# Converting six channel-mix weight parts before the last key/value batch is done, with part of its lerp and square work moved to DVE and three raw key/query tiles

## The chip, the cores and the metric

One NeuronCore of a Trainium2 chip runs the whole program. The metric is the device time of one execution in microseconds; the kernel before takes 1013.36 us (median of three runs, 1012.07 to 1013.84).

## What is computed

Three layers follow each other on a batch of 4, a sequence of 576 and 512 features: rotary attention with 8 heads, a channel mix with a gate, and a token mix followed by a wider channel mix.

```
q_rot, k_rot = rotate(q), rotate(k)
attn = softmax(q_rot @ k_rot^T / 8)
x    = attn @ v                                  # [4, 576, 512]

xk = mu_k * x + (1 - mu_k) * x_prev              # x_prev: x shifted by one position
xr = mu_r * x + (1 - mu_r) * x_prev
k  = relu(xk @ w_k)
y  = sigmoid(xr @ w_r) * ((k * k) @ w_v)         # [4, 576, 512]

h  = relu(y^T @ w_tok1) @ w_tok2                 # token mix, 576 -> 256 -> 576
u  = y + h^T
out = u + relu(u @ w_ch1) @ w_ch2                # channel mix, 512 -> 1536 -> 512
```

All weights arrive as 64-bit floats (read as pairs of 32-bit words), everything else as 32-bit floats.

## The kernel before, in words

**Precision.** Every operand of a large matmul is split into a high and a low half, both of type fp32r, and a product is three matmuls: high·high, high·low, low·high (`mm3`, L535 to L539). One matmul has 128 rows, 128 columns of weights and 288 columns of data (half a sequence), so that all units below come in halves `c` = 0, 1.

**Attention.** There are 16 groups `g` (4 batches, 4 head pairs) of 9 steps each, so 144 steps. A step makes scores (`emit_S`, L370), their maximum (L376, DVE), the exponential (L383, ACT), the normalized high half (L75, ACT) and low half (L402, DVE), and sends both through a DMA transpose (L417, L419) on the SP queue; twice per group the transposed tiles meet the values on PE (`emit_pv`, L432), and the result goes to `xT` (L82, DVE) and to memory `xd`. The raw key and query tiles, two of each per group (`rk`, `rq`, loaded by `ld_raw`, L263 and L266), are rotated in place on POOL and split (`split_hi`, `split_lo`). `BUFS` says how many raw tiles there are: 4 and 4.

**Key/value and gate units.** `kvr_gen` makes, for a batch and half, a K unit: four lerp slices (`lerp_slice`, one per 128 features), eight products `kp` with `w_k`, relu (`t`, L606, ACT), square (`k2`: high half L610 on ACT, `q` and the low half on POOL), and four products `vp` with `w_v`, whose results go to memory `vd`. An R unit makes four lerp slices and four products `rp` with `w_r`, the sigmoid (L650) and its multiplication into `y`. K units of batches 0 to 2 run between the steps of attention; then come, in this order (`SEQ`), K(3,0), R(0,0), R(0,1), K(3,1). A lerp slice is five instructions in a chain: `a` on POOL (L77), `f` scaled on ACT (L75), `f` plus `a` on POOL (L104), the high half `xs` on ACT (L73), the low half on POOL (L104). There is one buffer for `a`, one for `f`, four for `xs`.

**Weights.** `Conv` brings a part of a weight matrix (128 rows by 512 words of 64 bits, 512 KB; `w_tok1` 256 wide, `w_tok2` 576 wide) from memory to the place where its two halves will stand, and converts it by an absolute value on ACT (L191), four instructions on DVE (L196, L198, L200, L203), a copy to the high half on ACT (L73) and a subtraction for the low half on DVE (L104, written as `parts`). `conv0` does `w_k` and `w_v` during the first four groups of attention. `conv1` does `w_r` (4 parts), `w_tok1` (5), `w_tok2` (2). `conv2` does `w_ch1` and `w_ch2`, 12 parts each, in blocks of four.

**Where things lie.** The pools of attention (rk, rq, the rotation table, sp with the split keys and queries, and so on) are a stack on the right side of SBUF, opened in this order. When they are closed, the pools of the next stage (`top`: the three conversion buffers cv, then `w_r`, `w_tok1`, `w_tok2`, y, ...) are opened from the same end, so each takes the room of some attention pools and waits for the last reader there. The pools of the key/value stage (`wrk`, `kvs`) lie on the left.

**Order.** The program is written as generators that are advanced in turn; a scheduler then fixes each engine's instruction order ahead of the run, from priorities and its own estimates. On the chip each engine runs its list strictly in that order, and the SP queue issues its DMAs strictly in order too, so an instruction that waits holds up all behind it.

**The end.** After R(0,1), the token mix of batch 0 (`tok_gen`: `trp`, `ytk`, `t1p`, `t2p`) runs beside K(3,1). Then `ch_gen` does the channel mix of all batches (`uhl` splits, `c1p`, `hs`, `co`), with the gates and token mixes of batches 1 to 3 (`pre_gen`) in between. `PRE_FROM` and `PRE_EARLY` say from which channel item on, and how far per item, that work is advanced while weights are still being converted.

Of the kernel before, what the change touches and what calls it, by code (L numbers as in the profile page):

```python
# [33 lines left out]

SEQ = [("K", 3, 0), ("R", 0, 0), ("R", 0, 1), ("K", 3, 1)]

KVN, TKN, PRE, PRE_EARLY, PRE_FROM = 5, 6, 20, 6, 6

BUFS = dict(rk=4, rq=4, sp=2, vr=2, v16=2, p16=4, pt=2, sm=4, sc=3, la=1, lf=1, xs=4, t=2, q=2, vt=2)

PRI = dict(den=50, hi=400, pv=20, ld=-100, v=-50, low=50, rope=200, conv1=20, kv=-200, kvpe=-200)

# [22 lines left out]
def body(tc, kin, qin, vw, tabs, ident, mu, w_k, w_v, w_r, w_t1, w_t2, w_c1, w_c2, out):  # L65
# [37 lines left out]
    def tt(e, o, a, b, op):  # L103
        return (pool if e == "P" else dve).tensor_tensor(o, a, b, op=op)  # L104

    ctx = ExitStack()
    with ctx:
# [35 lines left out]
        def w3(w):  # L143
            return w.rearrange("(k p) f -> p k f", p=128)
# [377 lines left out]
        @prio("lerp")  # L522
        def lerp_slice(x, o, kk, w):
            a = P["a"].tile([128, HS], F32, tag="a", name="a")
            copy("P", a, x[:, kk, o:o + HS], om_s[:, w, kk:kk + 1])
            f = P["f"].tile([128, HS], F32, tag="f", name="f")
            copy("A", f, x[:, kk, o + 1:o + HS + 1], mu_s[:, w, kk:kk + 1])
            tt("P", f, f, a, ALU.add)
            t = P["xs"].tile([128, 2, HS], F32R, tag="xs", name="xs")
            copy("A", t[:, 0], f)  # L530
            tt("P", t[:, 1], f, t[:, 0].bitcast(F32), ALU.subtract)
            return t

        def mm3(p, w, m, t, first, last):
# [14 lines left out]
        def kvr_gen(seq, ready):  # L549
# [31 lines left out]
            for n, (kind, b, c) in enumerate(seq):  # L581
# [12 lines left out]
                if kind == "K":  # L594
                    k2 = [None] * KF
                    for m in range(KF):
                        p = accps("kp")
                        for kk in range(KD):
                            with ahead(PRI["kvpe"]):
                                mm3(p[:, 0:HS], wk[m // 4][kk], m % 4, xs[kk], kk == 0, kk == KD - 1)  # L600
                            tick()
                            yield 3

                        def ev1(p=p, m=m):
                            k2[m] = P["t"].tile([128, HS], F32, tag="t", name="t")
                            act.activation(out=k2[m], in_=p[:, 0:HS], func=AF.Relu)  # L606

                        def ev2(m=m):
                            t, k2[m] = k2[m], P["k2"].tile([128, 2, HS], F32R, tag="k2", name="k2")
                            act.activation(out=k2[m][:, 0], in_=t, func=AF.Square)  # L610
                            q = P["q"].tile([128, HS], F32, tag="q", name="q")
                            tt("P", q, t, t, ALU.mult)
                            tt("P", k2[m][:, 1], q, k2[m][:, 0].bitcast(F32), ALU.subtract)
                        later((1, ev1), (2, ev2))
                    load(n + 1)
                    for m in range(KD):
                        p = accps("vp")
                        for kf in range(KF):
                            with ahead(PRI["kvpe"]):
                                mm3(p[:, 0:HS], wv[kf // 4][kf % 4], m, k2[kf], kf == 0, kf == KF - 1)  # L620
                            if kf == 1:
                                load(n + 1)
                            if kf == 4:
                                lerp(n + 1)
                            tick()
                            yield 3

                        def ev(p=p, m=m, b=b, c=c):
                            vt = P["vt"].tile([128, HS], F32, tag="vt", name="vt")
                            copy("A", vt, p[:, 0:HS])  # L630
                            sp.dma_start(vd[b][c][:, m], vt)
                        later((1, ev))
                else:
                    load(n + 1)
                    y = u_of[b]
                    cc = slice(c * HS, (c + 1) * HS)
                    sp.dma_start(y[:, :, cc], vd[b][c])
                    for m in range(KD):
                        p = accps("rp")
                        for kk in range(KD):  # L640
                            with ahead(PRI["kvpe"]):
# [12 lines left out]
                        later((1, ev))  # L654
# [118 lines left out]
        def top(nm, bufs, st=mw):  # L773
            return st.enter_context(tc.tile_pool(name=nm, bufs=bufs, side="right"))
# [5 lines left out]
        y_p = [top("y0", 1)]  # L780
        M["ytk"], M["h1"] = top("m_ytk", 1), top("m_h1", 1)

        def cv_t():
            return cv_p.tile([128, S], I32, tag="cv", name="cv")

        cv = Conv(cv_t, [wr, t1, t2], "conv1", low="D")
        u_of[0] = y_p[0].tile([128, KD, S], F32, tag="y", name="y")
        for _ in range(3):
            cv.step()
# [1 line left out]
        while not kv.done:  # L791
            kv.advance(30)
            if not cv.done():
                cv.step()
            elif r_done:
                if tok is None:
                    tok = Stream(tok_gen(0))
                tok.advance(TKN)
# [6 lines left out]
        c1_w, c2_w = [], []
        for o in range(0, KC, 4):
            c1_w.append(Weights(top(f"c1{o}", 1), [w3(w_c1)[:, k, 128 * o:128 * o + 512] for k in range(KD)],
                                [128, 2, 512]))
            c2_w.append(Weights(top(f"c2{o}", 1), [w3(w_c2)[:, o + k] for k in range(4)], [128, 2, DM]))
# [5 lines left out]
        mi_p = mx.enter_context(tc.tile_pool(name="mi_p", bufs=2, space=PS))  # L815
        c1_p = mx.enter_context(tc.tile_pool(name="c1_p", bufs=2, space=PS))
        co_p = mx.enter_context(tc.tile_pool(name="co_p", bufs=4, space=PS))
        cv = Conv(cv_t, [w for ws in zip(c1_w, c2_w) for w in ws], "conv2", low="D")

        def gate_gen(b):  # L820

# [33 lines left out]
        def ch_gen():  # L855
# [3 lines left out]
            for n in range(len(items) + LAG):  # L859
# [18 lines left out]
                if n >= LAG:  # L878
                    b, c, kf = items[n - LAG]
                    h = hs_of.pop(n - LAG)  # L880
                    for m in range(KD):
                        if kf == 0:
                            co_of[m] = co_p.tile([128, 512], F32, tag="co", name="co")
                        mm3(co_of[m][:, 0:HS], c2_w[kf // 4][kf % 4], m, h, kf == 0, kf == KC - 1)
                    if kf == KC - 1:
                        cc = slice(c * HS, (c + 1) * HS)
                        for m in range(KD):
# [13 lines left out]
        while not ch.done:  # L901
# [73 lines left out]
```

## Time and profile before

| what | value |
|---|---|
| median of three runs | 1013.36 us (1012.07 to 1013.84) |
| the profiled execution's own time | 1011.27 us |
| its span in the trace | 1009.5 us |
| PE busy | 897.5 us, 89% of the span |
| DVE / ACT / POOL busy | 56% / 48% / 44% |
| mean granted TensorE clock | 0.949 |

A row of the timeline gives start, duration, engine, line, operation, output and inputs, and in brackets how long the engine had been idle and which instruction ended that. A row of the table by stretches gives, for each engine, its busy time in that stretch and in parentheses how many instructions began there, then the granted TensorE clock, the share of the DMA engines and what they moved. Matmuls overlap in the records (a record lasts 0.29 us, the next begins 0.13 us later), so a stretch with no idle time may still hold fewer matmuls than it could.

### The profile page before, as it was taken

How to read it: one execution, taken by the hardware profiler on the slowest of the kernel's cores; microseconds unless marked ns; L12 is line 12 of the kernel's file. 1: busy time of each engine (PE TensorE's matmuls, PEld its weight loads, DVE VectorE, ACT ScalarE, POOL GpSimd, SP SyncE). 2: the span in 40 equal slices, each digit the busy share in tenths (PEclk: the TensorE clock that was granted, in tenths of full speed). 3: DMA queues.
4: the chain of work that ended last, by engine and by line, in shares of the span. 5: the costliest groups of instructions: out<-in, count | busy, mean ns of one | idle time of the engine just before them, and what ended most of it. 6: DMA issues, size and time to landing. Idle time of an engine off the chain costs nothing.

```text
span 1009.5 us, 17679 instructions
## 1 busy us (share of the span) xinstructions
PE 897.5 (89%) x6544; PEld 822.2 (81%) x6544; DVE 566.3 (56%) x1237; ACT 487.9 (48%) x1088; POOL 445.5 (44%) x484
## 2 busy tenths in 40 slices
PE   2566578999998899989888888999999999999998
PEld 1454456788787788878787788999999999999997
DVE  5998987768677577796850199932223211231111
ACT  2665666767677586766554455541133112221110
POOL 6679866857768654452567731240141013101010
PEclk9965577999999999999999999999999999999999
DMA  7999888898788877687920283020120002000000
GB/s 252 289 269 237 163 167 169 184 182 174 177 176 173 156 133 149 153 191 134 215 95 24 67 314 148 13 60 1 39 62 22 21 2 77 1 24 15 10 25 24
DMA packets 212054, 120.80 MB, mean 120 GB/s; under 512 B 175232, under 2 KB 192768, under 8 KB 211840
## 3 DMA queue, kind: packets, MB, share of 16 engines
q1 hardware_dynamic: 211968, 119.67, 50.1%
q8 instruction: 52, 0.85, 0.4%
q14 instruction: 34, 0.28, 0.1%
HBM read 60.90 MB, written 14.16 MB: 74 GB/s over the span
## 4 chain that ended last, share of the span: by engine, by line
PE 55%; DVE 5%; DMA 3%; POOL 2%; ACT 2%; issue 1%; SPq 0%; DVEq 0%; POOLq 0%; ACTq 0%
PE c1p L537 5%; PE co L537 5%; PE c1p L538 5%; PE c1p L539 5%; PE co L538 5%; PE co L539 5%; PE S L370 4%; PE pv L432 2%; PE vp L537 2%; PE kp L537 2%; PE vp L538 2%; PE vp L539 2%; PE rp L537 1%; PE rp L538 1%; PE rp L539 1%; PE kp L539 1%
## 5 line engine op out<-in xcount | busy, mean ns | idle before, releaser
L370 PE MATMUL S<-kq 64*128 64x288 f32 (+1 forms) x864 | 154.4, 341 | 26.3 <-DVE p L402 18.0
L370 PEld LDWEIGHTS S<-kq 64*128 64x128 f32 (+1 forms) x864 | 123.9, 213 | 50.0 <-issue 26.3
L383 ACT ACTIVATE S<-S,nm 128x576 f32<-128x576 f32 x144 | 102.2, 713 | 66.9 <-DVE nm L376 66.1
L874 DVE SCALAR_TENSOR_TENSOR hs<-c1p,hs 128x288 fp32r<-128x288 f32 x96 | 43.8, 456 | 152.5 <-ACT hs L873 152.1
L376 DVE TENSOR_REDUCE nm<-S 128x1 f32<-128x576 f32 x144 | 106.6, 751 | 38.9 <-PE S L370 38.3
L402 DVE SCALAR_TENSOR_TENSOR p<-S,rc,p 128x576 f16<-128x576 f32 x144 | 114.3, 811 | 19.3 <-ACT p L75 17.7
L873 ACT ACTIVATE hs<-c1p 128x288 fp32r<-128x288 f32 x96 | 38.8, 409 | 171.0 <-PE c1p L539 167.7
L104 POOL TENSOR_TENSOR uhl<-y,uhl 128x288 fp32r<-128x288 f32 x32 | 26.4, 852 | 212.8 <-ACT uhl L73 212.5
L537 PE MATMUL c1p<-uhl,parts 128*128 128x288 f32 x384 | 114.6, 299 | 3.7 <-DVE y L104 3.7
L538 PE MATMUL c1p<-uhl,parts 128*128 128x288 f32 x384 | 114.4, 298 | 0.0
L539 PE MATMUL c1p<-uhl,parts 128*128 128x288 f32 x384 | 114.4, 299 | 0.0
L539 PE MATMUL co<-hs,parts 128*128 128x288 f32 x384 | 112.6, 296 | 0.0
L538 PE MATMUL co<-hs,parts 128*128 128x288 f32 x384 | 112.5, 296 | 0.0
L75 ACT ACTIVATE p<-S,rc 128x576 f16<-128x576 f32 x144 | 104.4, 749 | 13.4 <-ACT S L383 4.4
L537 PE MATMUL co<-hs,parts 128*128 128x288 f32 x384 | 107.7, 296 | 0.0
L537 PE MATMUL kp<-xs,parts 128*128 128x288 f32 x256 | 79.8, 322 | 14.6 <-ACT xs L73 7.3
L432 PE MATMUL pv<-pt,vh 128*64 128x256 f16 (+1 forms) x576 | 60.1, 333 | 31.5 <-DMA pt<-p 25.9
L537 PE MATMUL vp<-k,parts 128*128 128x288 f32 x256 | 79.1, 313 | 2.1 <-ACT vt L73 1.1
L538 PE MATMUL vp<-k,parts 128*128 128x288 f32 x256 | 78.0, 306 | 0.7 <-POOL k L104 0.7
L538 PE MATMUL kp<-xs,parts 128*128 128x288 f32 x256 | 76.5, 301 | 1.7 <-POOL xs L104 1.4
L539 PE MATMUL vp<-k,parts 128*128 128x288 f32 x256 | 77.8, 305 | 0.0
L104 POOL TENSOR_TENSOR q<-t 128x288 f32<-128x288 f32 x64 | 46.4, 729 | 68.9 <-ACT t L606 66.1
(115 smaller groups left out, 2362.5 us busy)
## 6 DMA issues: line engine op xcount, KB each, us to landing
words<-in_w_c_dram SPq DMA_DIRECT2D x24, 512.0 KB, 7.6
rq<-in_qin_dram SPq DMA_DIRECT2D x32, 320.0 KB, 3.6
rk<-in_kin_dram SPq DMA_DIRECT2D x32, 288.0 KB, 3.4
vr<-in_vw_dram SPq DMA_DIRECT2D x16, 320.0 KB, 3.5
xd<-xT SPq DMA_DIRECT2D x16, 288.5 KB, 3.1
vd<-vt SPq DMA_DIRECT2D x32, 144.0 KB, 2.1
y<-vd SPq DMA_DIRECT2D x8, 576.0 KB, 5.0
out_dram<-y SPq DMA_DIRECT2D x8, 576.0 KB, 3.6
```

Of the source, the lines that this page charges most:

```text
L75: act.activation(out=o, in_=i, func=AF.Copy, scale=scale)
L104: return (pool if e == "P" else dve).tensor_tensor(o, a, b, op=op)
L370: pe.matmul(p[:, h, 0:HS], lhsT=a[l, 128 * m:128 * m + 128], rhs=b[l, h * HS:(h + 1) * HS], start=(n == 0), stop=(n == 2))
L376: dve.tensor_reduce(out=nm, in_=S_t[j][:, :, 0:HS], op=ALU.max, axis=AX.XY, negate=True)
L383: act.activation(out=e, in_=e, func=AF.Exp, bias=sum_t[j], accum_out=s)
L402: dve.scalar_tensor_tensor(out=t[:, 1], in0=S_t.pop(j)[:, :, 0:HS], scalar=sum_t[j], in1=t[:, 0], op0=ALU.mult, op1=ALU.subtract)
L432: pe.matmul(p[l, 0:n], lhsT=v[:, a, l], rhs=ts[x][:, c, :], start=(i == 0), stop=(i == len(prods) - 1))
L537: pe.matmul(p, lhsT=wh, rhs=t[:, 0], start=first, stop=False)
L538: pe.matmul(p, lhsT=wh, rhs=t[:, 1], start=False, stop=False)
L539: pe.matmul(p, lhsT=wl, rhs=t[:, 0], start=False, stop=last)
L873: act.activation(out=h[:, 0], in_=p[:, 0:HS], func=AF.Relu)
L874: dve.scalar_tensor_tensor(out=h[:, 1], in0=p[:, 0:HS], scalar=0.0, in1=h[:, 0].bitcast(F32), op0=ALU.max, op1=ALU.subtract)
```

## The change

- `BUFS`: three raw key tiles and three raw query tiles in place of four and four.
- `lerp_slice`, when called after attention's program text (`second`): the scaling and the addition of `f` become one DVE instruction, and the low half of `xs` goes from POOL to DVE. This holds for R(0,0), R(0,1) and K(3,1), 12 slices.
- In K units evaluated after attention (K(3,0) and K(3,1)) the low half of `k2` goes from POOL to DVE: 16 instructions.
- The first block of `w_ch1` (4 parts) and the first two parts of `w_ch2` get pools in attention's room and are appended to `conv1`; `conv2` does the other 18. The token mix of batch 0 starts at the same point of `conv1`, and `needed` counts which parts a channel item wants, one item ahead.
- `PRE_EARLY`, `PRE_FROM` from 6, 6 to 10, 2.

```diff
-KVN, TKN, PRE, PRE_EARLY, PRE_FROM = 5, 6, 20, 6, 6
+KVN, TKN, PRE, PRE_EARLY, PRE_FROM, EARLY = 5, 6, 20, 10, 2, 2
-BUFS = dict(rk=4, rq=4, sp=2, ...
+BUFS = dict(rk=3, rq=3, sp=2, ...
...
             f = P["f"].tile([128, HS], F32, tag="f", name="f")
-            copy("A", f, x[:, kk, o + 1:o + HS + 1], mu_s[:, w, kk:kk + 1])
-            tt("P", f, f, a, ALU.add)
+            if second:
+                dve.scalar_tensor_tensor(out=f, in0=x[:, kk, o + 1:o + HS + 1], scalar=mu_s[:, w, kk:kk + 1], in1=a,
+                                         op0=ALU.mult, op1=ALU.add)
+            else:
+                copy("A", f, x[:, kk, o + 1:o + HS + 1], mu_s[:, w, kk:kk + 1])
+                tt("P", f, f, a, ALU.add)
...
-            tt("P", t[:, 1], f, t[:, 0].bitcast(F32), ALU.subtract)
+            tt("D" if second else "P", t[:, 1], f, t[:, 0].bitcast(F32), ALU.subtract)
...
-                            tt("P", k2[m][:, 1], q, k2[m][:, 0].bitcast(F32), ALU.subtract)
+                            tt("D" if second else "P", k2[m][:, 1], q, k2[m][:, 0].bitcast(F32), ALU.subtract)
...
+        c1_w = [c1_part(0)]
+        early = [c1_w[0], c2_part(0, EARLY)]
...
-        cv = Conv(cv_t, [wr, t1, t2], "conv1", low="D")
+        cv = Conv(cv_t, [wr, t1, t2] + early, "conv1", low="D")
...
-            elif r_done:
+            if r_done and cv.n >= 17:
...
-            while n < KC and cv.n < min(len(cv.q), 8 * (n // 4) + 5 + n % 4) + 6:
+            while n < KC - 1 and needed(n + 1) and cv.n < min(len(cv.q), needed(n + 1)) + 6:
```

**Where the order moves, 1.** The SP queue at the end of attention. Before, three parts of `w_r` (`words<-in_w_r`) stand among the transposes of group 13 and the fourth among those of group 14:

```order
L419 DMA_TRANSPOSE pt_5649<-p_5698 128x9x128
L183 DMA words<-in_w_r_dram 128x1024 x3
L419 DMA_TRANSPOSE pt_5701<-p_5741 128x9x128
L417 DMA_TRANSPOSE pt_5649<-p_5825 128x9x64
L417 DMA_TRANSPOSE pt_5701<-p_5825 128x9x64
L419 DMA_TRANSPOSE pt_5940<-p_5872 128x9x128
L419 DMA_TRANSPOSE pt_5989<-p_5937 128x9x128
L183 DMA words<-in_w_r_dram 128x1024
```

Now they stand among the last transposes of group 15, and the token and early channel parts follow:

```order
L419 DMA_TRANSPOSE pt_6478<-p_6494 128x9x128
L183 DMA words<-in_w_r_dram 128x1024 x2
L419 DMA_TRANSPOSE pt_6497<-p_6513 128x9x128
L183 DMA words<-in_w_r_dram 128x1024
L417 DMA_TRANSPOSE pt_6478<-p_6551 128x9x64
L417 DMA_TRANSPOSE pt_6497<-p_6551 128x9x64
L183 DMA words<-in_w_r_dram 128x1024
L183 DMA words<-in_w_t_dram 128x512 x5
L183 DMA words<-in_w_t_dram 128x1152 x2
L183 DMA words<-in_w_c_dram 128x1024 x4
L443 DMA xd_63<-xT 128x577
L183 DMA words<-in_w_c_dram 128x1024 x2
```

The pools cv and `w_r` take the first 23,296 bytes per partition of attention's room. With four raw tiles of each kind, rk, rq and the rotation table take 24,576; with three, 19,712, and `w_r` reaches into sp, which is read until the last score. All of `w_r` has moved behind attention, and two parts of `w_ch2` (the last row) have come ahead of K(3,1).

**Where the order moves, 2.** DVE between the first K unit of the last batch and the token mix. Before, the conversions (`parts`) are followed at once by the token mix (`ytk`):

```order
L200 SCALAR_TENSOR_TENSOR cv<-words,cv 128x512
L203 SCALAR_TENSOR_TENSOR cv<-words,cv 128x512
L104 TENSOR_TENSOR parts<-cv,parts 128x512 x2
L104 TENSOR_TENSOR ytk<-trp,ytk 128x256 x4
L834 SCALAR_TENSOR_TENSOR f<-x,mu_s,a 128x288
```

Now the low halves of K(3,0) and the first lerp slices stand between the last conversions, and ten more slices behind them:

```order
L203 SCALAR_TENSOR_TENSOR cv<-words,cv 128x512
L104 TENSOR_TENSOR parts<-cv,parts 128x512
L104 TENSOR_TENSOR k_6894<-q,k_6894 128x288
L104 TENSOR_TENSOR xs<-f,xs 128x288
L104 TENSOR_TENSOR parts<-cv,parts 128x512
L528 SCALAR_TENSOR_TENSOR f<-xT,mu_s,a 128x288
L104 TENSOR_TENSOR xs<-f,xs 128x288
L528 SCALAR_TENSOR_TENSOR f<-xT,mu_s,a 128x288
L104 TENSOR_TENSOR xs<-f,xs 128x288
L528 SCALAR_TENSOR_TENSOR f<-xT,mu_s,a 128x288
```

`k_6894` is the eighth and last low half of K(3,0); the first two slices of R(0,0) come out between conversions, the other two directly after the last one, so R(0,0) stands in DVE's list behind all 17 parts of `conv1`.

**Where the order moves, 3.** The SP queue between the second and the fourth transpose of group 0. Before, parts of `w_k` and `w_v` stand there:

```order
L419 DMA_TRANSPOSE pt_309<-p_279 128x9x128
L183 DMA words<-in_w_k_dram 128x1024 x2
L419 DMA_TRANSPOSE pt_282<-p_306 128x9x128
L355 DMA vh<-vh 64x512
L356 DMA vh<-vh 64x512
L183 DMA words<-in_w_k_dram 128x1024 x4
L274 DMA vr<-in_vw_dram 128x640
L183 DMA words<-in_w_v_dram 128x1024 x2
L419 DMA_TRANSPOSE pt_309<-p_327 128x9x128
```

Now there are fewer of them, and raw tiles of groups 2 and 3:

```order
L419 DMA_TRANSPOSE pt_282<-p_306 128x9x128
L183 DMA words<-in_w_k_dram 128x1024 x2
L355 DMA vh<-vh 64x512
L356 DMA vh<-vh 64x512
L183 DMA words<-in_w_k_dram 128x1024 x2
L266 DMA rq<-in_qin_dram 128x640
L274 DMA vr<-in_vw_dram 128x640
L263 DMA rk<-in_kin_dram 128x576 x2
L266 DMA rq<-in_qin_dram 128x640
L419 DMA_TRANSPOSE pt_309<-p_327 128x9x128
```

With the two parts at the head of the queue, the fourth transpose (`pt_309<-p_327`) has now six parts of weights ahead of it in place of ten, and four raw tiles, each of which needs a buffer that POOL or DVE must first free.

## Rows read from the trace of the kernel before

**Rows 1.** The page: busy time, and PE and DVE in 40 slices.

```profile
PE 897.5 (89%) x6544; PEld 822.2 (81%) x6544; DVE 566.3 (56%) x1237; ACT 487.9 (48%) x1088; POOL 445.5 (44%) x484
...
PE   2566578999998899989888888999999999999998
...
DVE  5998987768677577796850199932223211231111
```

**Rows 2.** Table by stretches: us, busy us per engine, PEclk, DMA share, GB/s.

```profile
397.20:422.70 25.50, 25.50 (x199) 21.66 (x198) 18.41 (x52) 17.61 (x39) 7.97 (x10) 1.00 0.71 140
422.70:459.30 36.60, 33.33 (x249) 29.10 (x250) 33.29 (x64) 26.18 (x58) 17.77 (x21) 0.95 0.82 187
480.20:536.20 56.00, 48.73 (x353) 46.24 (x352) 36.53 (x63) 30.00 (x70) 35.74 (x43) 0.97 0.50 138
536.20:542.60 6.40, 6.40 (x50) 6.40 (x49) 0.00 (x0) 4.34 (x10) 3.90 (x6) 1.00 0.27 95
542.60:567.00 24.40, 18.30 (x105) 14.04 (x104) 1.60 (x4) 10.43 (x25) 19.03 (x27) 1.00 0.08 24
567.00:612.00 45.00, 36.32 (x264) 35.12 (x263) 31.47 (x61) 24.87 (x58) 19.13 (x24) 0.96 0.70 259
612.00:650.00 38.00, 38.00 (x276) 38.00 (x276) 35.41 (x71) 20.20 (x39) 4.57 (x5) 0.96 0.08 31
```

**Rows 3.** Timeline of ACT and POOL, one lerp slice of R(0,1).

```profile
545.54 0.51 POOL L77 TENSOR_SCALAR a<-xT,om_s 128x288 f32<-128x288 f32 x1
...
546.84 0.54 ACT L75 ACTIVATE f<-xT,mu_s 128x288 f32<-128x288 f32 x1 [0.93 <-POOL xs L104]
...
548.29 0.44 ACT L73 ACTIVATE xs<-f 128x288 fp32r<-128x288 f32 x1 [0.91 <-POOL f L104]
548.82 0.80 POOL L104 TENSOR_TENSOR xs<-f,xs 128x288 fp32r<-128x288 f32 x1
549.65 0.54 ACT L75 ACTIVATE f<-xT,mu_s 128x288 f32<-128x288 f32 x1 [0.93 <-POOL xs L104]
```

**Rows 4.** Timeline of PE: two products of attention that waited for transposes.

```profile
47.23 2.13 PE L432 MATMUL pv<-pt,vh 128*64 128x256 f16 x17 [5.20 <-DMA pt<-p]
...
434.13 0.30 PE L432 MATMUL pv<-pt,vh 128*64 128x320 f16 x1 [3.17 <-DMA pt<-p]
```

**Rows 5.** Timeline of the SP queue: loads of `w_r`.

```profile
423.47 1.29 SPq L183 DMA_DIRECT2D words<-in_w_r_dram  x3
```

**Rows 6.** Timeline of DVE: first and last instruction of the conversions after attention.

```profile
485.73 0.29 DVE L196 TENSOR_SCALAR cv<-cv 128x256 f32<-128x256 f32 x1 [0.95 <-ACT cv L191]
...
521.41 0.69 DVE L104 TENSOR_TENSOR parts<-cv,parts 128x512 fp32r<-128x512 f32 x1
```

**Rows 7.** L196 on DVE from 482 to 523 us and from 625 to 650 us; L203 then.

```profile
L196 DVE TENSOR_SCALAR cv<-cv x11: 275/445/1060, 485.7 to 516.8; 128x256 f32<-128x256 f32 x5, 128x512 f32<-128x512 f32 x4, 128x576 f32<-128x576 f32 x2
...
L196 DVE TENSOR_SCALAR cv<-cv x8: 417/420/423, 625.8 to 647.1; 128x512 f32<-128x512 f32 x8
...
L203 DVE SCALAR_TENSOR_TENSOR cv<-words,cv x9: 679/684/687, 624.6 to 647.5; 128x512 int32<-128x512 int32 x9
```

**Rows 8.** Timeline of DVE and POOL: one kind of instruction beside POOL, and alone.

```profile
581.63 1.79 POOL L104 TENSOR_TENSOR k<-q,k 128x288 fp32r<-128x288 f32 x2
581.70 1.05 DVE L834 SCALAR_TENSOR_TENSOR f<-x,mu_s,a 128x288 f32<-128x288 f32 x1 [0.52 <-POOL xs L104]
583.79 0.45 DVE L104 TENSOR_TENSOR y<-t2p,y 128x288 f32<-128x288 f32 x1
586.53 0.51 DVE L834 SCALAR_TENSOR_TENSOR f<-x,mu_s,a 128x288 f32<-128x288 f32 x1
```

**Rows 9.** Timeline of PE: six transposes of the token mix.

```profile
554.66 1.12 PE L734 MATMUL trp<-idn,y 128*128 128x128 f32 x6
```

**Rows 10.** Loads of raw keys, and maxima of scores: duration min/median/max, first and last start.

```profile
L263 SPq DMA_DIRECT2D rk<-in_kin_dram x32: 327/426/727, 2.6 to 340.4; - x32
...
L376 DVE TENSOR_REDUCE nm<-S x144: 733/752/759, 19.3 to 480.3; 128x1 f32<-128x576 f32 x144
```

More of the change, by code (lines that the diff above doesn't have):

```diff
@@ L35 @@
 SEQ = [("K", 3, 0), ("R", 0, 0), ("R", 0, 1), ("K", 3, 1)]
-KVN, TKN, PRE, PRE_EARLY, PRE_FROM = 5, 6, 20, 6, 6
-BUFS = dict(rk=4, rq=4, sp=2, vr=2, v16=2, p16=4, pt=2, sm=4, sc=3, la=1, lf=1, xs=4, t=2, q=2, vt=2)
+KVN, TKN, PRE, PRE_EARLY, PRE_FROM, EARLY = 5, 6, 20, 10, 2, 2
+BUFS = dict(rk=3, rq=3, sp=2, vr=2, v16=2, p16=4, pt=2, sm=4, sc=3, la=1, lf=1, xs=4, t=2, q=2, vt=2)
 PRI = dict(den=50, hi=400, pv=20, ld=-100, v=-50, low=50, rope=200, conv1=20, kv=-200, kvpe=-200)
@@ L781, in body, with c1_part, c2_part @@
         M["ytk"], M["h1"] = top("m_ytk", 1), top("m_h1", 1)
+        def c1_part(o):
+            return Weights(top(f"c1{o}", 1), [w3(w_c1)[:, k, 128 * o:128 * o + 512] for k in range(KD)], [128, 2, 512])
+        def c2_part(o, n):
+            w = Weights(top(f"c2{o}", 1), [w3(w_c2)[:, o + k] for k in range(n)], [128, 2, DM])
+            c2_at.update({o + k: (w, k) for k in range(n)})
+            return w
+        c2_at = {}
+        c1_w = [c1_part(0)]
+        early = [c1_w[0], c2_part(0, EARLY)]
         def cv_t():
             return cv_p.tile([128, S], I32, tag="cv", name="cv")
-        cv = Conv(cv_t, [wr, t1, t2], "conv1", low="D")
+        cv = Conv(cv_t, [wr, t1, t2] + early, "conv1", low="D")
         u_of[0] = y_p[0].tile([128, KD, S], F32, tag="y", name="y")
@@ L804, in body @@
         ps.close()
[L805 to L809, printed above, removed]
+        late = [c2_part(EARLY, 4 - EARLY)]
+        for o in range(4, KC, 4):
+            c1_w.append(c1_part(o))
+            late += [c1_w[-1], c2_part(o, 4)]
         mx = ExitStack()
@@ L817, in body, with needed @@
         co_p = mx.enter_context(tc.tile_pool(name="co_p", bufs=4, space=PS))
-        cv = Conv(cv_t, [w for ws in zip(c1_w, c2_w) for w in ws], "conv2", low="D")
+        cv = Conv(cv_t, late, "conv2", low="D")
+        def needed(kf):
+            return max(kf - EARLY + 1, 0) if kf < 4 else 8 * (kf // 4) - 8 + (4 - EARLY) + 5 + kf % 4
         def gate_gen(b):
@@ L883, in ch_gen @@
                             co_of[m] = co_p.tile([128, 512], F32, tag="co", name="co")
-                        mm3(co_of[m][:, 0:HS], c2_w[kf // 4][kf % 4], m, h, kf == 0, kf == KC - 1)
+                        mm3(co_of[m][:, 0:HS], c2_at[kf][0][c2_at[kf][1]], m, h, kf == 0, kf == KC - 1)
                     if kf == KC - 1:
```

## The prediction

> **What bounds the kernel now.** I read the page first [rows 1]: PE is busy for 89% of the span and at 9 from the 26th slice on. What is to be had lies where its digit is lower: the first seven slices, two single ones, and slices 18 to 25, some 430 to 630 us. DVE there stands at 5 to 9, then at 0 and 1 (22nd and 23rd slice), then at 9: its work is badly spread, not too much. The table by stretches [rows 2] says what the holes cost. From 536.2 to 542.6 us PE does 50 matmuls in 6.40 us, 0.128 us each; this is its pace when nothing is late. From 542.6 to 567.0 it does 105 in 24.4 us. In those 24.4 us DVE is busy for 1.6 us and POOL for 19.0. From 612 us, where the first `c1p` runs, to 650 PE has no hole [rows 2], and the page shows 9 and once 8 behind that; the change alters none of the matmuls, so the end moves by what the first `c1p` moves.
>
> The timeline of ACT and POOL shows the hole's cause [rows 3]: a lerp slice goes ACT, POOL, ACT, POOL, and since there is one buffer `f` the next begins when the last low half is done, 2.81 us later (549.65 less 546.84). PE has 12 matmuls per slice, 1.54 us. Eight slices, of R(0,1) and K(3,1), run like this.
>
> Two more places count. Group 14 of attention takes 36.6 us for 249 matmuls, group 13 25.5 us for 199 [rows 2]; at the pace of group 13 (7.8 per us) it would take 31.9, so 4.7 us are lost. The group holds a wait of 3.17 us of PE for a transpose [rows 4], some 10 us after three loads of `w_r` were put on the same SP queue [rows 5], and all of `w_r`'s conversion: DVE is busy for 33.3 of 36.6 us, after 18.4 of 25.5 [rows 2]. And from the last score (its matmuls end at 480.2) to the first `rp` (536.2) PE needs 56.0 us, with DVE converting from 485.73 to 522.1 [rows 2, 6].
>
> **The change, part by part.**
>
> *Three raw tiles, steady state: 0.* The last raw key is loaded at 340.4 us, while the 16 groups run from 19.3 to 480.3 us, 28.8 us each, so the last group begins at about 451 [rows 10]: raw tiles are some 110 us ahead. One tile fewer costs one group of that lead, and 80 us remain to hide a load.
>
> *Three raw tiles, the start: 0, between −5 and +5 us.* The fourth transpose has fewer weights and more raw tiles before it on SP, which wait for buffers. Its product waited 5.20 us on PE at 47.23 [rows 4], and the next scores stand behind that product. That wait may go, or come once more; I take the middle, since it is the same 16 parts that pass, and only their place differs.
>
> *`w_r` behind attention: −4.7 us, then given back.* The loss in group 14 should go (at worst none of it). PE's list now has six `kp` products of K(2,1) behind the last score where it had three: 36 matmuls, 4.6 us, only moved. So the last score should end at 480.2 − 4.7 − 4.6 = 470.9. With the same stalls PE would then reach the first `rp` at 470.9 + 56.0 + 4.6 = 531.5. But DVE has more to do. Its first conversion came 5.5 us behind the last score, which now makes 476.4. Before, 11 parts (5 of 256 columns, 2 of 576, 4 of 512: 4480 columns) took from 485.73 to 522.10 [rows 6], 36.4 us or 8.1 ns a column, with POOL busy beside it and the same instruction taking from 0.28 to 1.06 us. With POOL nearly idle, L196 takes 0.42 and nine parts of 512 pass in 25 us [rows 7], 5.4 ns a column. Now it is 17 parts, 7552 columns: 41 to 61 us. I take 6.8 ns, 51.4 us, since POOL is busy with K(2,1) and K(3,0)'s slices in the first half and loses its low halves in the second. Between the conversions stand eight low halves of K(3,0) at 0.45 (the nearest row, a DVE addition of 288 columns) and two slices at 0.51 + 0.45 [rows 8]: 5.5 us. Two slices follow, 3.1 us. Sum: 476.4 + 51.4 + 5.5 + 3.1 = 536.4. DVE, not PE, then sets the first `rp`, at 536.4 where it was 536.2: **+0.2 us**, between −4.7 (PE's own 531.5) and +9.9 (61 us of conversion).
>
> *Slices on DVE: −8.0 us.* The chain of a slice becomes 0.51 (DVE) + 0.44 (ACT) + 0.45 (DVE) with three hand-overs of some 0.06 [rows 3, 8]: 1.58 us, as long as PE's 1.54. `a` (0.51, [rows 3]) is made on POOL while the high and low halves are made. ACT loses an instruction per slice. Eight slices make 12.6 us, eight transposes at 1.12/6 [rows 9] 1.5, and 1.2 are needed once, because the first slice of R(0,1) wants a buffer that R(0,0)'s last product frees: 15.3 in place of 24.4 us, −9.1. At best PE alone counts (96 × 0.128 + 1.5 = 13.8, so −10.6). At worst DVE and POOL never work together: eight slices need DVE for 7.7 us, and POOL for eight `a` at 0.51 and up to eight of the gate's multiplications at 0.80 (its rate in [rows 3]), 10.5 us, which with the 1.2 makes 19.4, so −5.0. They do hinder each other: the same `f` took 1.05 us beside a POOL subtraction and 0.51 alone, but a DVE addition at 583.79 took its 0.45 [rows 8]. I put in 1.1 us of such waits: −8.0. DVE has room otherwise: by its list the conversions end before this stretch, and it did 1.6 us here.
>
> The Trainium skill (SBUF — State Buffer, section "Who interferes with whom") says that a DVE instruction with two inputs in SBUF and a GpSimd instruction that reads SBUF exclude each other, the later one waiting until the other is done. The row of the 1.05 us agrees. By that rule alone this term would go to its worst end, −5.0, as the moved instructions have two inputs in SBUF.
>
> *Token mix and K(3,1)'s second half, 567 to 612 us: −1 us (−3 to +1).* PE lacks 45.0 − 264 × 0.128 = 11 us here, mostly behind DVE, which is busy for 31.5 of 45 [rows 2]. The low halves of `k2` cost DVE 0.45 each and spare POOL; the conversion of 18 parts begins at the same point of the order as that of the rest did. The last chain (`t2p`, `y`, `uhl`, `c1p`) is unchanged.
>
> *Two parts of `w_ch2` earlier, `PRE_EARLY`, `PRE_FROM`: 0.* They feed a stretch in which PE is busy for 38.0 of 38.0 us although DVE converts for 35.4 of them [rows 2]. The cover is PE's own backlog of gate products; if it went, item 2 would wait for one part, 2.8 us.
>
> Sum: 0 + 0.2 − 8.0 − 1 = −8.8 us. The profiled execution took 1011.27 us (a span of 1009.5 and 1.8 around it), 2.1 below the median of 1013.36. So 1002.5 for its like, **1004.6 us** for the median.
>
> **Rivals.**
>
> *DVE is the new bound (slower).* If POOL and DVE keep each other waiting all along, conversion takes 61 us, the first `rp` comes at 546 (+9.9), slices gain only 5.0 and the token mix loses 1: +5.9, median 1019.3. It decides once the first `rp` is later than 541 to 545 us, where the delay has eaten the 5.0 to 8.0 + 1 us gained behind it. For it: 1.06 us for an instruction that takes 0.42 [rows 7]. Against: with the slices gone from it POOL has little to do while the last third of the parts is converted, only K(3,0)'s `q` and the next `a`.
>
> *More than forecast.* If DVE keeps to 5.4 ns a column it is done by 526, PE sets the first `rp` (−4.7), slices reach −10.6, the token mix −2: −17.3, median 996.1. For it: by the counts of [rows 2], at 0.128 us a matmul, PE lacks 33 us from 480 to 612. Against: K(3,0)'s slices stay on POOL.
>
> *The start eats it.* If SP, waiting for a raw buffer, makes the transposes late at the first two group boundaries by the 5.20 us of [rows 4] each, +10.4 meets −8.8: +1.6, median 1015.0, within what counts as the same. For it: the scores stand behind those products on PE. Against: the raw tiles asked for there are freed by rotations that POOL does early.
>
> **How the numbers follow.** Forecast 0.50, more than forecast 0.23, the start 0.13, DVE the bound 0.14. A measurement of this kernel can't tell 0.2%, 2 us, from no change. Nearly all of the forecast (0.49), the second rival (0.23) and a little of the third (0.03) are faster: 0.75. Same: 0.11, most of it the third. Slower: 0.14, nearly all the first rival. The range runs from 994, the far side of the second rival, to 1016, beyond the third; it leaves out the far part of the first.
>
> **What would show it.** Right: group 14 at about 32 us; PE doing some 105 matmuls of R(0,1) and K(3,1) in 16 to 17 us; `f` on DVE at about 0.51; first `c1p` at about 603. The prediction is wrong in its main step if slices still come 2 us or more apart, in its second if the first `rp` is off 536 by over 5 us, and in its cover if PE shows holes after the first `c1p`.

## The result, and the profile after

The changed kernel takes 1004.97 us (median of 20 runs, 1000.29 to 1010.96), the kernel before 1013.71 (20 runs): a ratio of 0.9903, 95% interval 0.9882 to 0.9924. That is 8.7 us less; the forecast was 8.8 less. Single executions of the changed kernel spread over some 10 us. Most of such a difference can lie in attention: two profiles of one kernel below (the change with four raw tiles), 2.87 us apart as a whole, have their last score 2.52 us apart. The profiled execution of the change took 1009.67 us, so its stretches are read, not its total.

The page of the changed kernel, busy times and then PE, DVE and the granted clock in 40 slices (before: [rows 1]):

```profile
PE 901.0 (89%) x6544; PEld 829.5 (82%) x6544; DVE 588.5 (58%) x1277; ACT 480.4 (48%) x1076; POOL 416.6 (41%) x444
...
PE   2557687989999999999789998999999999999997
...
DVE  6989978767677767666896599642124211232111
...
PEclk9966556989999999999999998999999999999999
```

POOL lost 40 instructions and DVE gained 40. DVE's 22nd and 23rd slices, before 0 and 1, are 6 and 5, and PE's slices 22 to 24 (before 8) are 9; the 20th, behind the last groups of attention, is 7.

The table by stretches of the changed kernel: groups 13, 14 and 15 of attention (the last one up to the end of the last score's matmuls), then up to the first `rp`, up to the first `c1p`, and behind it:

```profile
397.90:426.20 28.30, 28.30 (x223) 24.84 (x224) 17.99 (x45) 18.56 (x42) 9.48 (x13) 1.00 0.67 131
426.20:452.00 25.80, 24.99 (x196) 21.49 (x196) 18.28 (x41) 19.08 (x44) 14.01 (x19) 1.00 0.64 120
452.00:476.57 24.57, 24.34 (x200) 21.41 (x200) 16.01 (x37) 16.59 (x39) 5.95 (x9) 1.00 0.95 190
476.57:544.02 67.45, 56.59 (x392) 53.05 (x393) 61.11 (x108) 37.36 (x84) 33.69 (x37) 0.95 0.49 161
544.02:608.68 64.66, 57.79 (x415) 55.45 (x413) 43.70 (x87) 35.33 (x82) 23.40 (x30) 0.97 0.49 176
608.68:650.00 41.32, 41.32 (x293) 41.32 (x294) 35.89 (x68) 21.28 (x44) 9.71 (x9) 0.93 0.14 45
```

The same in the kernel before, group 15 and the two long stretches:

```profile
459.30:480.24 20.94, 20.94 (x163) 17.37 (x162) 13.99 (x31) 13.79 (x32) 7.33 (x10) 1.00 0.75 129
480.24:536.21 55.97, 48.70 (x352) 46.21 (x352) 36.53 (x63) 29.98 (x70) 35.74 (x43) 0.97 0.50 138
536.21:611.79 75.58, 60.80 (x415) 55.34 (x413) 32.87 (x64) 39.62 (x92) 42.06 (x56) 0.98 0.46 169
```

The gain is plain in the last: the same 415 matmuls in 64.66 us in place of 75.58. Between the last score and the first `rp` PE has 40 matmuls more and needs 11.5 us more. Behind the first `c1p` there is no hole, and from it to the last matmul PE takes 394.0 us where it took 392.7; over all runs below this part is 392.7 to 394.0, so whatever a run gains or loses it does ahead of that point.

The timeline of DVE in the changed kernel, slices of R(0,1) (start, duration; `f`, then the low half of `xs`):

```profile
552.70 0.52 DVE L528 SCALAR_TENSOR_TENSOR f<-xT,mu_s,a 128x288 f32<-128x288 f32 x1 [0.41 <-POOL a L77]
553.73 0.46 DVE L104 TENSOR_TENSOR xs<-f,xs 128x288 fp32r<-128x288 f32 x1 [0.51 <-ACT xs L73]
554.29 0.52 DVE L528 SCALAR_TENSOR_TENSOR f<-xT,mu_s,a 128x288 f32<-128x288 f32 x1
555.32 0.46 DVE L104 TENSOR_TENSOR xs<-f,xs 128x288 fp32r<-128x288 f32 x1 [0.51 <-ACT xs L73]
555.88 0.52 DVE L528 SCALAR_TENSOR_TENSOR f<-xT,mu_s,a 128x288 f32<-128x288 f32 x1
```

The next `f` starts 1.59 us after the last one (554.29 less 552.70), where a slice came every 2.81 us [rows 3]. This is the pace of slices that nothing disturbs. The seven `f` from 550.79 to 562.59 start 1.91, 1.59, 1.59, 2.33, 2.63 and 1.75 us apart, 1.97 in the mean; the seven from 543.96 to 563.15 in the kernel before come 3.20 apart in the mean.

### The profile page after: what moved, and what is told of

Same layout as the page of the kernel before. It is cut to its first block, busy times and chain, and to the rows that moved or that the text cites. A ratio compares the mean times of both kernels' runs of the same rounds, so it can differ in the third digit from the quotient of the medians.

```text
span 1007.9 us, 17696 instructions
## 1 busy us (share of the span) xinstructions
PE 901.0 (89%) x6544; PEld 829.5 (82%) x6544; DVE 588.5 (58%) x1277; ACT 480.4 (48%) x1076; POOL 416.6 (41%) x444
## 4 chain that ended last, share of the span: by engine, by line
PE 53%; DVE 6%; DMA 2%; ACT 1%; issue 1%; POOL 0%; SPq 0%; DVEq 0%; POOLq 0%; ACTq 0%
PE c1p L541 5%; PE co L541 5%; PE c1p L542 5%; PE c1p L543 5%; PE co L542 5%; PE co L543 5%; PE S L370 3%; PE rp L541 2%; PE vp L541 2%; PE pv L432 2%; PE rp L542 2%; PE rp L543 2%; PE vp L542 2%; PE vp L543 2%; PE kp L541 1%; DVE cv L203 1%
## 5 line engine op out<-in xcount | busy, mean ns | idle before, releaser
L370 PE MATMUL S<-kq 64*128 64x288 f32 (+1 forms) x864 | 157.4, 345 | 24.8 <-DVE p L402 11.7
L370 PEld LDWEIGHTS S<-kq 64*128 64x128 f32 (+1 forms) x864 | 128.1, 218 | 52.1 <-issue 24.9
L541 PE MATMUL c1p<-uhl,parts 128*128 128x288 f32 x384 | 115.2, 301 | 3.7 <-DVE y L104 3.7
L541 PE MATMUL co<-hs,parts 128*128 128x288 f32 x384 | 108.1, 297 | 0.0
L541 PE MATMUL kp<-xs,parts 128*128 128x288 f32 x256 | 80.6, 324 | 9.8 <-ACT t L610 8.1
L541 PE MATMUL vp<-k,parts 128*128 128x288 f32 x256 | 79.9, 314 | 2.6 <-ACT t L610 1.3
```

The lines of the kernel that those rows point to most:

```text
L370: pe.matmul(p[:, h, 0:HS], lhsT=a[l, 128 * m:128 * m + 128], rhs=b[l, h * HS:(h + 1) * HS], start=(n == 0), stop=(n == 2))
L541: pe.matmul(p, lhsT=wh, rhs=t[:, 0], start=first, stop=False)
```

## Which part of the change does it

Two parts can be separated: the number of raw tiles, which decides where `w_r` is loaded and converted (with three behind attention, with four beside its groups 13 and 14), and who makes the slices. Four runs on one chip fill the square. The rival theories are named in the expectations.

**Slices back on ACT and POOL**, all else as in the change:

```diff
-            if second:
-                dve.scalar_tensor_tensor(out=f, ...)
-            else:
-                copy("A", f, ...)
-                tt("P", f, f, a, ALU.add)
+            copy("A", f, ...)
+            tt("P", f, f, a, ALU.add)
...
-            tt("D" if second else "P", t[:, 1], f, ...)
+            tt("P", t[:, 1], f, ...)
```

> The change with the lerp slices after attention back on ACT and POOL (f in two steps, low half of xs on POOL); the low halves of k2 stay on DVE. Theory S (the slices bring the gain, the place of w_r nothing net): the stretch from the first rp to the first c1p goes from 64.7 us back to 73 to 76, the time is 8 to 11 us above the change's 1005.0, so 1013 to 1016, ratio to the kernel before 0.999 to 1.002. Theory W (w_r's place behind attention brings it, the slices only fill a wait that DVE's conversions would leave anyway): 1004 to 1007, ratio 0.990 to 0.993. Theory E (early channel parts and PRE numbers): also 1004 to 1007.

**Slices alone**: the kernel before with only those lines of the change.

> The kernel before with nothing changed but the lerp slices after attention (f as one DVE instruction, low half of xs on DVE). Theory S: first rp at its old distance of 56.0 us from the last score, first rp to first c1p 64 to 67 us in place of 75.6, time 1003 to 1006, ratio 0.990 to 0.992. Theory W or E: 1012 to 1014, ratio 0.998 to 1.002.

**Four raw tiles** in the change:

```diff
-BUFS = dict(rk=3, rq=3, ...
+BUFS = dict(rk=4, rq=4, ...
```

> The change with four raw tiles of each kind again, which puts w_r's loads and conversion back beside groups 13 and 14 of attention. Theory S: what group 14 loses (5 to 10 us) comes back at the first rp, which stands some 56 to 60 us behind the last score in place of 67.4; time 1002 to 1008, ratio 0.988 to 0.995. Theory W: the gain goes, 1011 to 1015, ratio 0.998 to 1.002. Theory E: 1003 to 1007, as theory S.

**Three raw tiles alone**: the kernel before with the opposite edit.

> The kernel before with three raw tiles of each kind and nothing else, so that w_r moves behind attention while the slices stay on ACT and POOL. Theory S: group 14 falls from 36.6 us to 26 to 32, the first rp stands 62 to 67 us behind the last score in place of 56.0, time 1011 to 1016, ratio 0.998 to 1.003. Theory W: 1003 to 1007, ratio 0.990 to 0.994. Theory E: 1011 to 1016, as theory S.

Measured (ratios to the kernel before with their 95% intervals; stretches from each profile, in us; S is the end of the last score):

| run | time | ratio | S to first `rp` | `rp` to `t1p` | `t1p` to `c1p` |
|---|---|---|---|---|---|
| before | 1014.29 | 1 | 55.97 | 31.10 | 44.48 |
| three raw tiles alone | 1015.89 | 1.0017 (0.9998 to 1.0035) | 66.26 | 31.12 | 45.69 |
| the change, slices back | 1015.39 | 1.0011 (0.9991 to 1.0031) | 66.96 | 30.98 | 43.26 |
| slices alone | 1004.25 | 0.9896 (0.9867 to 0.9926) | 55.47 | 22.14 | 43.68 |
| the change, four raw tiles | 1002.78 | 0.9885 (0.9853 to 0.9918) | 56.25 | 22.14 | 42.33 |
| the change | 1004.97 | 0.9903 (0.9882 to 0.9924) | 67.45 | 22.13 | 42.53 |

The slices on DVE bring the whole gain, with `w_r` at either place: theory S holds in all four runs, W and E fall. The place of `w_r` brings nothing: it costs 1.6 us in the first pair (1015.89 less 1014.29) and 2.2 in the second (1004.97 less 1002.78, not measured together), neither beyond its interval. The early channel parts with the low halves of `k2` show only between `t1p` and `c1p`, at −1.3 to −2.4 us (42.33 less 43.68; 43.26 less 45.69).

## Why the slices were slow

**Two buffers f**, in the kernel before, slices still on ACT and POOL:

```diff
-BUFS = dict(..., la=1, lf=1, ...
+BUFS = dict(..., la=1, lf=2, ...
```

> The kernel before with two buffers f in place of one and nothing else; the slices stay on ACT and POOL. Theory 'the single buffer' (the slice is a chain of four hand-overs, the next one waits for the buffer): POOL no longer waits 0.65 us per slice for ACT's f, the cycle falls from 2.81 us to POOL's own 0.51 + 0.80 + 0.80 = 2.11, first rp to first c1p from 75.5 to about 70.5, time 1008 to 1010, ratio 0.994 to 0.997. Theory 'POOL is full' (with the gate's multiplications its load alone makes the pace): 0 to -1.5 us, ratio 0.998 to 1.001.

1009.06 us, ratio 0.9941 (0.9920 to 0.9962); `rp` to `t1p` 27.30 us in place of 31.10, `t1p` to `c1p` 40.21 in place of 44.48 (from the last score to the first `rp` this profile needs 60.9 us, with 377 matmuls there). The timeline of POOL in this run:

```profile
546.08 0.80 POOL L104 TENSOR_TENSOR f<-f,a 128x288 f32<-128x288 f32 x1
546.98 0.51 POOL L77 TENSOR_SCALAR a<-xT,om_s 128x288 f32<-128x288 f32 x1
547.45 0.81 POOL L104 TENSOR_TENSOR xs<-f,xs 128x288 fp32r<-128x288 f32 x1
548.22 0.80 POOL L104 TENSOR_TENSOR f<-f,a 128x288 f32<-128x288 f32 x1
549.12 0.51 POOL L77 TENSOR_SCALAR a<-xT,om_s 128x288 f32<-128x288 f32 x1
```

POOL no longer waits within a slice, and the cycle is 2.14 us (548.22 less 546.08), POOL's own work. So the single buffer was a cause, worth 3.8 us in the slices (31.10 less 27.30), and POOL's load the next one. The order of the instructions shifted with the buffer, and the 4.3 us between `t1p` and `c1p` are not explained by it; 2.0 of them are a shorter wait ahead of the first `c1p` (last section).

**Only f on DVE**, in the kernel before; the low half of `xs` stays on POOL.

> The kernel before with only f made by one DVE instruction in slices after attention; the low half of xs stays on POOL. By the chain the cycle is 0.52 (DVE) + 0.44 (ACT) + 0.80 (POOL) and three hand-overs of 0.06, 1.94 us in place of 2.81: eight slices save 7.0, so 64 to 70 us from the first rp to the first c1p and 1006 to 1008, ratio 0.992 to 0.995. Rival, DVE and POOL hinder each other (f on DVE beside POOL's low half takes 1.05 and the low half longer): cycle 2.4 us or more, gain under 3.5, ratio over 0.9965.

1004.34 us, less than the 1006 to 1008 expected, ratio 0.9900 (0.9873 to 0.9927); `rp` to `t1p` 25.23 us. DVE and POOL in this run:

```profile
542.81 0.52 DVE L528 SCALAR_TENSOR_TENSOR f<-xT,mu_s,a 128x288 f32<-128x288 f32 x1 [1.42 <-POOL xs L104]
544.75 0.52 DVE L528 SCALAR_TENSOR_TENSOR f<-xT,mu_s,a 128x288 f32<-128x288 f32 x1 [1.42 <-POOL xs L104]
```

```profile
543.43 0.51 POOL L77 TENSOR_SCALAR a<-xT,om_s 128x288 f32<-128x288 f32 x1 [0.65 <-DVE f L528]
543.90 0.81 POOL L104 TENSOR_TENSOR xs<-f,xs 128x288 fp32r<-128x288 f32 x1
```

The cycle is 1.94 us, as worked out from the chain. The rival falls here: `f` takes 0.52, since in this chain DVE and POOL take turns. Two of the eight `f` of this stretch do meet one of the gate's multiplications on POOL and take 1.11 and 0.73 us.

**The change with four raw tiles, only f on DVE** (low halves of `xs` and `k2` on POOL again), beside the change and its four-tile form, each once more:

```diff
-            tt("D" if second else "P", t[:, 1], f, ...)
+            tt("P", t[:, 1], f, ...)
...
-                            tt("D" if second else "P", k2[m][:, 1], ...)
+                            tt("P", k2[m][:, 1], ...)
```

> The same with the low halves of xs and of k2 back on POOL, so that only f is on DVE. If f alone is the gain, as e6_f_only says: first rp to first c1p 66 to 69 us in place of 64.5, and the time within 0 to +3 us of the run with four raw tiles, ratio 0.988 to 0.992. If the moved low halves are what frees the slices: 70 us or more from the first rp to the first c1p and 1007 to 1010.

> The change with four raw tiles (w_r back beside attention), once more beside the change. Theory 'w_r behind attention costs a little' (the stalls it brings behind the last score outweigh what group 14 gains): 2 to 4 us below the change. Theory 'given back exactly' (my prediction's +0.2): within 1 us of it.

> The change itself once more, beside the next run on the same chip: 1003 to 1007, ratio 0.989 to 0.993. It gives a second profile of it, since the first was one of its slower executions: the stretch from the last score to the first rp again 66 to 68 us with some 392 matmuls, from the first rp to the first c1p 64 to 66.

| run | time | ratio | S to first `rp` | `rp` to `t1p` | `t1p` to `c1p` |
|---|---|---|---|---|---|
| the change again | 1004.14 | 0.9900 (0.9863 to 0.9937) | 67.67 | 22.14 | 42.30 |
| four raw tiles again | 1002.51 | 0.9892 (0.9857 to 0.9927) | 56.15 | 22.13 | 42.34 |
| four raw tiles, only f | 1010.36 | 0.9962 (0.9942 to 0.9982) | 56.54 | 25.21 | 44.74 |

The last run missed its expectation of 0 to +3 us: it is 7.9 above its like. From the first `rp` to the first `c1p` it takes 69.95 us against 64.47: 3.1 of the 5.5 are in the slices (25.21 less 22.13), as in the run before, and 2.4 in the token mix, where a `t1p` waits 4.58 us for DVE's `ytk`. So in the stretch of the slices the low halves on DVE are a second, smaller gain: with `f` alone the slices give 5.9 us (31.10 less 25.2), with both 9.0. The whole time shows that gain in this pair only. In the kernel before, `f` alone measured 1004.3 and both 1004.25, each against the kernel before on its own chip; the stretches of the run with `f` alone (−5.9 and −1.6 us) would make a ratio of about 0.993, at the edge of its interval. Why the two pairs differ stays open. Of the other two runs, the change again did as expected; the form with four raw tiles came out 1.6 us below it, between its two theories.

## What `w_r` behind attention costs

In the timeline of the changed kernel PE reaches the first `rp` without a wait, straight from the last `vp`. DVE ended its last conversion at 539.3 and the last low half of R(0,0)'s slices at 542.4, both ahead of it:

```profile
538.62 0.68 DVE L104 TENSOR_TENSOR parts<-cv,parts 128x512 fp32r<-128x512 f32 x1
...
541.96 0.46 DVE L104 TENSOR_TENSOR xs<-f,xs 128x288 fp32r<-128x288 f32 x1 [0.64 <-ACT xs L73]
```

```profile
543.88 0.29 PE L543 MATMUL vp<-k,parts 128*128 128x288 f32 x1
544.02 0.29 PE L541 MATMUL rp<-xs,parts 128*128 128x288 f32 x1
```

So PE, not DVE, sets the first `rp`. With three raw tiles alone DVE has 10.5 us less to do in that stretch, and it is nearly as long:

```profile
476.56:542.82 66.26, 55.07 (x393) 51.37 (x393) 50.60 (x81) 35.74 (x83) 44.54 (x51) 0.97 0.45 144
```

The 11.5 us more from the last score to the first `rp` are, by the two tables: 40 matmuls, 5.1 us at 0.128; 3.6 of PE idle (67.45 less 56.59 makes 10.86, before 7.27); and 2.8 in matmuls that stand further apart, at a granted clock of 0.95 in place of 0.97. The second profile of the change (the change again, above) splits its 11.7 us otherwise, 5.0 for 39 matmuls, 2.2 of idle and 4.5 of spacing, at a clock of 0.92:

```profile
476.49:544.16 67.67, 58.16 (x391) 54.20 (x392) 61.02 (x108) 37.49 (x84) 34.46 (x37) 0.92 0.49 160
```

Some of the idle time lies where the timeline of PE in the first profile shows it, with ACT's below it:

```profile
482.97 0.40 PE L541 MATMUL kp<-xs,parts 128*128 128x288 f32 x1 [1.84 <-ACT t L610]
...
493.61 0.40 PE L541 MATMUL kp<-xs,parts 128*128 128x288 f32 x1 [1.95 <-ACT t L610]
```

```profile
481.96 0.66 ACT L191 ACTIVATE cv<-words 128x512 f32<-128x512 f32 x1 [0.86 <-DMA words<-in_w_r_dram]
482.52 0.40 ACT L610 ACTIVATE t<-kp 128x288 f32<-128x288 f32 x1
...
492.63 0.63 ACT L73 ACTIVATE parts<-cv 128x512 fp32r<-128x512 f32 x1 [0.77 <-DVE cv L203]
493.17 0.39 ACT L610 ACTIVATE t<-kp 128x288 f32<-128x288 f32 x1
```

Each `kp` of K(2,1) needs the one accumulator bank that `t` empties, and `t` stands in ACT's list behind conversion steps that wait for `w_r`'s load or for DVE. Six such products now follow the last score, where three did. But the kernel before has such waits too, one of 0.56 us and this one (L537 there is L541 in the change):

```profile
486.74 0.61 PE L537 MATMUL kp<-xs,parts 128*128 128x288 f32 x1 [2.49 <-ACT t L606]
```

So the waits of K(2,1)'s `kp` grow from 3.05 us to 4.35 (0.56, 1.84 and 1.95) in the first profile of the change and to 3.86 (0.56, 2.07 and 1.23) in the second, some 1 us. The rest of the additional idle time lies further on, most of it in waits of K(3,0)'s `kp`.

Two runs were to give these products more banks of PSUM, three of four in turn from the score tiles, once the last scores are written:

```diff
-            if second and n_acc[0] % 4:
+            if (second or n_acc[1]) and n_acc[0] % 4:
...
+            n_acc[1] = j >= NTT - 2
             a_step(j, kv.advance)
```

> e3_four_raw (the change with four raw tiles) in which the key/value products issued once the last score is out may use the score banks of PSUM, three of four in turn, where they had one accumulator bank. Theory 'the one bank makes kp wait for t': the idle times of 0.56 and 2.74 us behind the last score go, the first rp comes about 3 us earlier and the time is 999 to 1001, 2 to 4 us below e3_four_raw. Rival 'DVE's conversions are the bound behind it': the first rp stays at 56 us behind the last score and the time within 1.5 us of e3_four_raw (1002.8).

> The change itself with the same use of the score banks. Theory 'one bank': the waits of 0.56, 1.84 and 1.95 us of kp for t behind the last score go, first rp 63 to 65 us behind the last score in place of 67.4, time 1001 to 1003, 2 to 4 us below the change's 1005.0. Theory 'DVE bounds the first rp' (my prediction's step): no change of the first rp, 1004 to 1006.

They measured 1000.36 us (0.9877, 0.9850 to 0.9904; on four raw tiles) and 1006.38 (0.9919, 0.9892 to 0.9945; on the change), each within its like's interval. They decide nothing: the waits are still there (0.56 and 2.24 us in the first, 0.56 and 1.96 in the second), since a product gets its bank where the program writes it, and K(2,1)'s `kp` are written 14 and more steps ahead of the edit's point. The next products are written behind attention, where `second` gave them these banks before. So the edit moves no product to another bank, and the two runs are further runs of the two kernels; that the first came out within the 999 to 1001 of its theory 'one bank' is chance. Whether the bank or ACT's order is the better lever was not tried further.

One more thing tells three raw tiles from four, far ahead. From 130 to 260 us PE begins 781 to 807 matmuls in the five profiles with three raw tiles, and 823 to 849 in the eight with four. The table by stretches for the change and for its form with four raw tiles:

```profile
130.00:260.00 130.00, 113.73 (x786) 95.02 (x786) 95.21 (x217) 82.84 (x184) 84.51 (x83) 0.84 0.86 169
```

```profile
130.00:260.00 130.00, 116.13 (x825) 95.61 (x825) 95.96 (x224) 87.60 (x195) 90.78 (x91) 0.88 0.85 172
```

Some 40 matmuls, 5 us of PE's work at 0.128, are left for later; the granted clock is 0.82 to 0.87 in the first five and 0.88 to 0.91 in the others. The clock does not hold them back; they stand later in PE's list, which is fixed ahead of the run. Ahead of the first score of group 6 PE has done 84 key/value matmuls in all five profiles with three raw tiles, and 113 in seven of the eight with four (96 in the one with two buffers `f`). When group 13 begins, at 396 us in the kernel before and 397 in the change, both have done 384 `kp`, but the `vp` differ (first before, then the change):

```profile
0.00:396.00 396.00, 57.85 (x360) 51.95 (x360) 6.18 (x15) 0.89 0.88 192
```

```profile
0.00:397.00 397.00, 49.48 (x312) 44.94 (x312) 5.16 (x13) 0.87 0.88 191
```

So 48 matmuls, 6.1 us of PE's work, are missing there without attention being any earlier. Why the scheduler orders them so with three raw tiles, and how far the lower clock follows from the fewer matmuls, stays open.

## Why the prediction was right, point by point

**What bounds.** Right: from the first `c1p` to the last matmul every run needs 392.7 to 394.0 us, and no hole opened behind it. That `c1p` came at 608.7 in the profile, where 603 was to show it; the profiled execution is 4.7 us above its median, so this decides nothing.

**Slices, −8.0 (−10.6 to −5.0).** Right in mechanism, a little small. From the first `rp` to the first `t1p` PE needs 22.13 us in place of 31.10: −9.0. The table by stretches, first the products of R(0,0), then those of R(0,1) and K(3,1):

```profile
544.02:550.42 6.40, 6.40 (x51) 6.40 (x50) 0.53 (x1) 3.21 (x6) 2.37 (x3) 1.00 0.14 49
550.42:566.15 15.73, 15.05 (x108) 13.95 (x107) 9.35 (x19) 6.70 (x19) 8.00 (x12) 1.00 0.11 33
```

108 matmuls in 15.73 us, where some 105 in 16 to 17 were to show it and 24.4 were needed before [rows 2]. The 1.1 us put in for DVE and POOL hindering each other was too much. They do meet, and one pair shows in an `f` of 0.87 us beside three of the gate's multiplications that took 2.74:

```profile
557.00 2.74 POOL L104 TENSOR_TENSOR y<-q,y 128x288 f32<-128x288 f32 x3
```

```profile
558.21 0.87 DVE L528 SCALAR_TENSOR_TENSOR f<-xT,mu_s,a 128x288 f32<-128x288 f32 x1
```

A second `f` took 0.68 us and two low halves 0.80 and 0.83, each beside such a multiplication; the other six low halves took 0.46 or 0.47, and the other six `f` 0.52, since what POOL then does, `a`, is done before `f` begins. So the sign set for being wrong, slices 2 us or more apart, was met by two of the six distances (2.33 and 2.63) and missed by their mean (1.97), while PE waited only 0.68 us in the whole stretch (15.73 less 15.05). Two readings behind this term were off. The addition that kept its 0.45 us [rows 8] has one input in a matmul's output, `t2p`, and so does not stand for the low halves, which read two tiles in SBUF. The 1.06 us of [rows 7] belong to an L196 of 576 columns, and the other of that width took 0.45; the four of 512 columns took 0.41 to 0.90, and only to these does the 0.42 compare. By the Trainium skill (SBUF — State Buffer, section "Who interferes with whom") alone the term would have come out at its worst end, −5.0; the trace agrees with the rule where the two meet (0.87 for 0.52), but only four of the sixteen moved instructions were lengthened.

**Token mix, −1 (−3 to +1).** −2.0 (42.53 less 44.48): inside its range.

**`w_r` behind attention, +0.2 at the first `rp`.** This is the step that was mis-sized, and its mechanism was wrong too. Group 14 lost its stall as said: groups 14 and 15 run 396 matmuls in 50.37 us, 7.9 per us, where they ran 412 in 57.54, 7.2 per us [rows 2]; the 5.1 us that this makes (412 at 7.86 per us are 52.4) stand beside the 4.7 forecast. But the last score ended at 476.6, not 470.9, and the first `rp` came at 544.0, not 536.4, more than the 5 us off that were to show this step wrong. "DVE, not PE, then sets the first `rp`" fell: the conversions took 58.1 us (481.20 to 539.30), about the 51.4 + 5.5 worked out, and PE came later still. PE's own 531.5 was 12.5 us short. Of these, 5.7 lie ahead of the last score: I had its end come 4.6 us earlier for the 36 matmuls that move behind it, but the matmuls that are missing there (984 `kp` and `vp` ahead of the last score in place of 1022) are put off before group 13 already, where this saved no time. The other 6.8 lie behind it, where I had taken "the same stalls": 0.5 in four matmuls more than the 36, 3.6 in idle time and 2.8 in matmuls further apart at a lower clock. The net cost is some 2 us. Three raw tiles were slower than four in all four comparisons, by 1.6 us in the kernel before, by 2.2 and 1.6 in the change, and by 6.0 between the two runs with the spare banks; no single one resolves it.

**Three raw tiles.** At the start 0 was right: the wait for a transpose stands at 44.84 with 4.33 us where it had 5.20 [rows 4], and PE begins 359 to 377 matmuls up to 130 us in the five profiles with three tiles, 376 to 384 in the eight with four, hence a few less. "Steady state: 0" was too simple: some 40 matmuls fall behind between 130 and 260 us, because PE's list has them later.

**Early parts, `PRE_EARLY`: 0.** Nothing against it: PE is full behind the first `c1p`.

So the 8.8 came out as 8.7 by two misses that met: the slices and token mix gave some 11 us in place of 9, and `w_r`'s new place took about 2 in place of 0.2. Of the rivals, "DVE is the new bound" had its late first `rp` (beyond 541) but not its reason, and slices that gave 9 rather than 5 kept the result on the other side. "The start eats it" left no clear trace: the wait at the first group boundary was 0.87 us shorter. The −17.3 of "more than forecast" wanted PE to be free of stalls behind the last score, which was its weakest point.

**A better form.** The change with four raw tiles keeps all of the gain and leaves `w_r` beside attention: 1002.78 and 1002.51 us (0.9885, 0.9892), lower than the change both times, though the intervals overlap. The run at 1000.36 us (0.9877), in effect the same kernel, points the same way.

## What to carry to other kernels

Where a short chain over several engines shares one buffer, take its cycle from the timeline and cut the longest hand-over first: one DVE instruction in place of two on ACT and POOL gave two thirds of the slices' gain in their stretch, and the cycle of its undisturbed slices was worked out to the hundredth beforehand. When work moves behind another stage, count the matmuls between two landmarks before saying who arrives last, and look at whose evictions will stand in the queue behind the moved work. Matmuls that leave a stretch save time only if PE was what that stretch waited for. A term that is taken as zero because loads are early may still move the order of everything else: compare counts by stretch, in more than one profile.

## What was not expected of the hardware

Ahead of the first `c1p` PE idles 3.7 to 3.9 us in twelve of the thirteen profiles, and the chain shows a DVE queue, not a computation. The change's DVE, with POOL's splitting of `uhl` beside it, and PE:

```profile
604.89 1.18 DVE L104 TENSOR_TENSOR y<-t2p,y 128x288 f32<-128x288 f32 x3
605.99 1.25 DVE L203 SCALAR_TENSOR_TENSOR cv<-words,cv 128x512 int32<-128x512 int32 x1
607.15 1.01 DVE L196 TENSOR_SCALAR cv<-cv 128x512 f32<-128x512 f32 x1
608.09 0.45 DVE L104 TENSOR_TENSOR y<-t2p,y 128x288 f32<-128x288 f32 x1
```

```profile
605.89 1.99 POOL L104 TENSOR_TENSOR uhl<-y,uhl 128x288 fp32r<-128x288 f32 x2 [11.55 <-ACT uhl L73]
```

```profile
608.68 0.58 PE L541 MATMUL c1p<-uhl,parts 128*128 128x288 f32 x1 [3.73 <-DVE y L104]
```

The last `y` stands behind two conversion steps that take 1.25 and 1.01 us beside POOL, where the same instructions take 0.68 and 0.42 [rows 7]: L196 has one input in SBUF and is held up too. PE's product waits for that `y`, although its own operand was ready at 607.9 (605.89 plus 1.99) at the latest; that it needs the bank which `y` empties is an inference. The thirteenth profile, with two buffers `f`, is in line with it: there one conversion step of 0.68 us stands ahead of the last pair of `y`, and PE idles 1.70 us. Moving that `y` ahead by hand was not tried.
